# Hashed attention with a maxout feed-forward: four heads per transposed tile, scores in 32-row rounds

## The chip, the cores and the metric

The kernel runs on one core of a Trainium2 chip. The time is that of the device for one launch, in microseconds (us); each kernel was run several times. Engines: PE is TensorE (matmuls), PEld its weight loads, DVE is VectorE, ACT is ScalarE, POOL is GpSimd, SP issues DMAs. A run is called slow when it is over 1.5% above the fastest of the same kernel; ratios use fast runs alone. A ratio is the mean time of one kernel's fast runs over the mean time of the kernel before in the same rounds on the same chip, so it is not quite the ratio of the medians that stand beside it.

## The reference, cut to what matters

```python
# q, k, v: (4 batches, 8 heads, 768, 64), proj: (64, 6)
q_bits = (q @ proj) > 0; k_bits = (k @ proj) > 0      # six bits a row
mask   = all six bits of the two rows agree
scores = where(mask, q @ k.T / 8, -1e9); attn = softmax(scores) @ v
x = attn of all heads side by side                     # (3072, 512)
h = max(x @ w1, x @ w2, x @ w3); out = h @ w_out       # 768 hidden, 512 out
```

## The kernel before

A batch has two groups of four heads (`pp`), and each group two halves of 384 queries: four phases a batch, 16 in all. A phase has six groups `c` of 128 keys. In each, PE makes the scores of four heads, and one more matmul a head adds a large negative number wherever the hash bits differ. ACT takes the exp. In the next phase PE sums the exps (`den`) and multiplies them by v (`av`). Feed-forward pieces of the batch before (`l1`, `l2`) are put between the groups. PSUM is the memory that PE writes its results to, and it is used in banks. The program gives a bank out anew once another engine has read out what stood in it. `scp` holds three tiles of two PSUM banks each for the scores, and `wkp` holds two PSUM banks for all that isn't scores or hash bits: `den`, `av`, `l1` and `l2` take turns in them.

```python
    scp = ... tile_pool(name="scp", bufs=3, space=PSUM)   # scores, two banks each
    wkp = ... tile_pool(name="wkp", bufs=2, space=PSUM)   # all else, one bank each

    def qk_group(ph, b, pp, half, c):
        for jj in (0, 1):                        # two heads a tile: 64 rows each
            for hd in (0, 1):
                nc.tensor.matmul(sc[:, hd, 0:HS], kT[D*hd : D*hd+D, ...], qT[D*hd : D*hd+D, ...],
                                 start=True, stop=False)
        for jj in (0, 1):
            for hd in (0, 1):                    # hash bits: 32 rows each
                nc.tensor.matmul(scs[jj][:, hd, 0:HS], bits["k", b, pp][32*g : 32*g+32, ...],
                                 bits["q", b, pp][32*g : 32*g+32, ...], start=False, stop=True)
        ... nc.scalar.activation(..., ActFn.Exp, scale=SCALE)

    def den(ph, b, pp, half):
        ... # 24 matmuls with ones into one bank
        nc.vector.tensor_scalar(out=ds[:], in0=ps[:, 0:HS], ...)       # frees the bank
        nc.vector.transpose(dT..., ds[:]); nc.vector.reciprocal(rc[:], dT[:, :, 0])
        for jj in (0, 1):
            ... nc.gpsimd.tensor_copy(r2[o : o+32, :], rc[s : s+32, :])   # four of them
            nc.vector.transpose(rb..., r2[:, :, None].to_broadcast(...))  # waits for GpSimd
            rcb[ph, jj] = rb                     # used by av, three groups later

    def l1(b, half, fb, m):
        ... # four matmuls into one bank
        if m == 0: nc.scalar.copy(h[:], ps[:, 0:HS])
        else:      nc.vector.tensor_tensor(out=h[:], in0=h[:], in1=ps[:, 0:HS], op=AluOp.max)
```

The softmax here doesn't subtract the row's maximum and nothing guards it: scores larger than these inputs give would overflow.

## Time and profile before

| stage (by the first exp of each batch) | us |
|---|---|
| launch to the first exp | 24.8 |
| batch 0 | 59.2 |
| batches 1, 2 and 3 to the last exp | 103.2 + 88.4 + 54.4 = 246.0 |
| last exp to the end | 45.1 |
| span of the profiled run | 375.1 |
| median of 2 runs | 377.82 |

The stages are read from the timeline of the 192 exp instructions, 48 a batch. The last stage holds a burst of 15 us of feed-forward as well, since the last exp comes before it.

### The profile page before, as it was taken

The numbers are of one execution on the slowest core, as the hardware profiler recorded it, in microseconds if no ns is written. First come the engines' busy times: TensorE is split into PE (matmuls) and PEld (weight loads), VectorE is DVE, ScalarE is ACT, GpSimd is POOL, SyncE is SP. The second block draws the span as 40 slices with busy tenths as digits, with TensorE's granted clock in tenths as the row PEclk, the third lists the DMA queues.
The fourth block names the chain that finished last, engine by engine and source line by source line (L and its number), as shares of the span: only waits on it lengthen the run. The fifth ranks groups of instructions, "written<-read, shape, count | busy, mean of one in ns | idle before, by whom it ended". The sixth has DMA issues, their size and how long they took to land.

```text
span 375.1 us, 6377 instructions
## 1 busy us (share of the span) xinstructions
PE 304.2 (81%) x2512; PEld 125.8 (34%) x2512; DVE 177.9 (47%) x301; ACT 182.6 (49%) x265; POOL 40.4 (11%) x178
## 2 busy tenths in 40 slices
PE   1278868678989879699988986399989889999796
PEld 0012323223433333235433432134533333345352
DVE  3330857864342576644234448825423535343451
ACT  1037658425657552242377664243276676642122
POOL 8000311101030111000013020100010010100100
PEclk9995799989999996899989999789998999999999
DMA  8999999994032970010199931010020000010202
GB/s 194 234 235 237 237 239 235 235 232 78 2 42 96 232 130 1 2 56 31 56 238 226 230 59 21 0 59 28 2 87 0 2 0 2 33 54 7 78 1 85
DMA packets 16414, 37.64 MB, mean 100 GB/s; under 512 B 2816, under 2 KB 9216, under 8 KB 16384
## 3 DMA queue, kind: packets, MB, share of 16 engines
q1 hardware_dynamic: 9600, 30.94, 33.5%
q0 software_dynamic: 6784, 6.30, 10.8%
q8 instruction: 19, 0.31, 0.4%
q14 instruction: 11, 0.09, 0.1%
HBM read 37.23 MB, written 6.29 MB: 116 GB/s over the span
## 4 chain that ended last, share of the span: by engine, by line
PE 52%; DMA 21%; DVE 14%; issue 6%; POOL 3%; ACT 2%; SPq 1%; DVEq 0%; POOLq 0%; ACTq 0%
DMA qnat<-in_q_dram 21%; PE wk L255 20%; PE wk L269 8%; PE wk L238 7%; PE sc L184 6%; PE wk L210 4%; PE sc L192 4%; PE bps L160 2%; DVE dT L216 1%; DVE ds L214 1%; DVE xT L245 1%; DVE kb L167 1%; SPq L75 1%; ACT at_145 L197 1%; DVE rc L218 1%
## 5 line engine op out<-in xcount | busy, mean ns | idle before, releaser
L255 PE MATMUL wk<-xT,w_sb 128*128 128x384 f16 x576 | 111.9, 330 | 18.9 <-DVE h_1691 L264 3.7
L255 PEld LDWEIGHTS <-w_sb 128*128 128x128 f16 x576 | 52.1, 98 | 71.5 <-issue 34.6
L192 PE MATMUL sc<-qb,kb 32*128 32x384 bf16 x384 | 34.7, 351 | 1.1 <-DVE qb L167 1.1
L214 DVE TENSOR_SCALAR ds<-wk 128x384 f32<-128x384 f32 x16 | 8.9, 558 | 50.3 <-PE wk L210 50.3
L272 ACT COPY o<-wk 128x512 f32<-128x512 f32 x24 | 14.1, 586 | 36.1 <-PE wk L269 29.6
L242 DVE TENSOR_SCALAR sv<-wk 128x1 f32<-128x1 f32 x32 | 5.0, 157 | 47.1 <-PE wk L238 47.1
L238 PEld LDWEIGHTS <-v 128*64 128x64 f16 x384 | 20.5, 116 | 14.2 <-issue 6.4
L197 ACT ACTIVATE at_137<-sc 128x768 f16<-128x768 f32 x8 | 6.6, 823 | 28.8 <-PE sc L192 28.5
L192 PEld LDWEIGHTS <-kb 32*128 32x128 bf16 x384 | 9.9, 92 | 31.5 <-issue 31.5
L197 ACT ACTIVATE at_181<-sc 128x768 f16<-128x768 f32 x8 | 6.5, 815 | 16.3 <-PE sc L192 16.3
L210 PEld LDWEIGHTS <-ones_131 128*32 128x32 f16 x384 | 9.7, 101 | 13.4 <-issue 9.9
L83 POOL DMA_DIRECT2D v<-in_v_dram x16 | 11.5, 726 | 19.0 <-PE wk L238 19.0
L167 DVE TENSOR_SCALAR qb<-bps,thrq 128x768 bf16<-128x768 f32 x8 | 7.9, 1015 | 10.1 <-PE bps L160 10.1
L197 ACT ACTIVATE at_153<-sc 128x768 f16<-128x768 f32 x8 | 6.5, 814 | 10.6 <-PE sc L192 10.6
L197 ACT ACTIVATE at_173<-sc 128x768 f16<-128x768 f32 x8 | 6.5, 814 | 7.6 <-PE sc L192 7.5
L197 ACT ACTIVATE at_165<-sc 128x768 f16<-128x768 f32 x8 | 6.5, 814 | 7.2 <-PE sc L192 7.2
L160 PE MATMUL bps<-kT_185,pmk 64*32 64x384 f32 x8 | 3.0, 843 | 8.3 <-DVE kT_185 L142 8.3
L216 DVE STREAM_TRANSPOSE dT<-ds 128x384 f32<-128x384 f32 x16 | 9.3, 578 | 0.6
L197 ACT ACTIVATE at_177<-sc 128x768 f16<-128x768 f32 x8 | 6.5, 815 | 4.7 <-PE sc L192 4.6
L197 ACT ACTIVATE at_141<-sc 128x768 f16<-128x768 f32 x8 | 6.5, 814 | 4.6 <-PE sc L192 4.6
L184 PE MATMUL sc<-qT_191,kT_189 64*128 64x384 bf16 x24 | 5.3, 430 | 3.9 <-ACT at_165 L197 0.6
L160 PE MATMUL bps<-kT_189,pmk 64*32 64x384 f32 x8 | 2.8, 844 | 6.9 <-DVE kT_189 L142 6.9
(526 smaller groups left out, 681.5 us busy)
## 6 DMA issues: line engine op xcount, KB each, us to landing
knat<-in_k_dram SPq DMA_DIRECT2D x64, 188.0 KB, 8.0
qnat<-in_q_dram SPq DMA_DIRECT2D x64, 188.0 KB, 8.0
out_dram<-o SPq DMA_DIRECT2D x24, 256.0 KB, 2.0
v<-in_v_dram POOLq DMA_DIRECT2D x16, 192.0 KB, 11.0
w_sb<-in_moe_w_dram POOLq DMA_DIRECT2D x3, 768.0 KB, 45.0
wo_sb<-in_moe_w_out_dram POOLq DMA_DIRECT2D x1, 768.0 KB, 72.1
pr<-in_proj_dram POOLq DMA_DIRECT2D x2, 1.5 KB, 4.1
```

The lines of the kernel that those rows point to most:

```text
L160: nc.tensor.matmul(pst[pp][32 * g : 32 * g + 32, half, 0:HS], pm[nm][D * hd : D * hd + D, :], tr[nm, b, 2 * pp + jj][D * hd : D * hd + D, ...
L167: nc.vector.tensor_scalar(out=t[:].rearrange("p (a n) -> p a n", a=2), in0=pst[pp][:, :, 0:HS], scalar1=thr[nm][:, 0:1], scalar2=(1.0 if n ...
L184: nc.tensor.matmul(sc[:, hd, 0:HS], kT[D * hd : D * hd + D, c * P : c * P + P], qT[D * hd : D * hd + D, half * HS : half * HS + HS], start ...
L192: nc.tensor.matmul(scs[jj][:, hd, 0:HS], bits["k", b, pp][32 * g : 32 * g + 32, c * P : c * P + P], bits["q", b, pp][32 * g : 32 * g + 32, ...
L197: nc.scalar.activation(atile(ph, jj, c)[:, :, 0:HS], scs[jj][:, :, 0:HS], ActFn.Exp, scale=SCALE)
L210: nc.tensor.matmul(ps[32 * g : 32 * g + 32, 0:HS], ones32[:], atile(ph, jj, c)[:, hd, 0:HS], start=(c == 0), stop=(c == NCH - 1))
L214: nc.vector.tensor_scalar(out=ds[:], in0=ps[:, 0:HS], scalar1=float(S) * EPS, scalar2=None, op0=AluOp.add)
L216: nc.vector.transpose(dT[:].rearrange("p a x -> p (a x)"), ds[:])
L238: nc.tensor.matmul(ps[D * hd : D * hd + D, 0 : HS + 1], vv[:, hd, c, :], atile(ph, jj, c)[:, hd, :], start=(c == 0), stop=(c == NCH - 1))
L255: nc.tensor.matmul(ps[:, 0:HS], w_sb[m][:, jc, fb * P : fb * P + P], xT[b][:, jc, half * HS : half * HS + HS], start=(jc == 0), stop=(jc = ...
L269: nc.tensor.matmul(ps[:, 0:DM], hts[b, half, fb][:, t * P : t * P + P], w_sb[3][:, fb, :], start=(fb == 0), stop=(fb == NFB - 1))
L272: nc.scalar.copy(o[:], ps[:, 0:DM])
```

## The change

The intent: four heads share one transposed tile, each head in one group of 32 rows, with its 64 numbers in two rounds; the hash bits are a third round of the same form. So all twelve matmuls of a score group have one form. The tile is loaded as it lies in memory, once. Seven parts of it are told apart below: loads halved; a quicker start (half loads, and 14 dummy matmuls while they run); what follows from these for batch 0; 32-row rounds; transposes spread over slots; the first of three maxima copied by DVE; and all PSUM banks used at the end.

```diff
-                nc.sync.dma_start(t[32*g : 32*g+32, 0 : R*D-32], s[:, 32*blk : 32*blk + R*D-32])   # x4 a pair of heads
+            nc.sync.dma_start(t[:], src)                       # four heads, once; halves for the first tile
-    nc.gpsimd.dma_start(pr[0:D, :], proj[:, :])
-    nc.gpsimd.dma_start(pr[D : 2*D, :], proj[:, :])
+    for g in range(4):
+        nc.scalar.dma_start(pr[32*g : 32*g+32], proj.rearrange("(a d) n -> d a n", a=2))
...
+        for rnd in range(3):
+            for g in range(4):
+                rows = slice(32*g, 32*g+32)
+                if rnd < 2: l, r = kT[rows, rnd, ks], qT[rows, rnd, qs]
+                else:       l, r = bits["k", b, pp][rows, ks], bits["q", b, pp][rows, qs]
+                nc.tensor.matmul(scs[g//2][:, g%2, 0:HS], l, r, start=(rnd == 0), stop=(rnd == 2))
...
     def bank():
+        if tail["on"]:
+            m = tail["i"] % 4
+            if m == 1: tail["t"] = scp.tile([P, 2, 512], ...); return tail["t"][:, 0, :]
+            if m == 2: return tail["t"][:, 1, :]
         return wkp.tile([P, 512], FP32, tag="wk", name="wk")[:]
...
-            nc.scalar.copy(h[:], ps[:, 0:HS])
+            if tail["on"]: nc.scalar.copy(h[:], ps[:, 0:HS])
+            else:          nc.vector.tensor_copy(h[:], ps[:, 0:HS])
...
-    (transposes of the next batch: four in a row at two places)
+            slots = [(1, 4), (1, 5), (2, 1), (2, 5), (3, 0), (3, 1), (3, 2), (3, 3)]   # (phase, group), one each
```

The hash now runs on 32 x 32 tiles, up to sixteen at once. To let them, three of four results come out shifted by whole groups of 32 rows, and small DMAs from SBUF to SBUF shift them back.

More of the change, by code (lines that the diff above doesn't have):

```diff
@@ L49 @@
     konst = ctx.enter_context(tc.tile_pool(name="konst", bufs=1))
-    natp = ctx.enter_context(tc.tile_pool(name="natp", bufs=4))
+    natp = ctx.enter_context(tc.tile_pool(name="natp", bufs=2))
     tp = ctx.enter_context(tc.tile_pool(name="tp", bufs=3))
@@ L66, with load @@
     nat = {}
-    def load_pair(b, j):
-        for nm, src in (("k", k), ("q", q)):
-            t = natp.tile([P, R * D], FP32, tag=nm + "nat", name=nm + "nat")
-            for hd in (0, 1):
-                for blk in (0, 1):
-                    g = 2 * hd + blk
-                    s = src[b, 2 * j + hd].rearrange("(i r) d -> i (r d)", r=R)
-                    nc.sync.dma_start(t[32 * g : 32 * g + 32, 0 : R * D - 32],
-                                      s[:, 32 * blk : 32 * blk + R * D - 32])
-            nat[nm, b, j] = t
+    def load(nm, b, pp, half=None):
+        src = {"k": k, "q": q}[nm][b, 4 * pp : 4 * pp + 4].rearrange("h (i r) d -> (h i) (r d)", r=R)
+        if (nm, b, pp) not in nat:
+            nat[nm, b, pp] = natp.tile([P, R * D], FP32, tag=nm + "nat", name=nm + "nat")
+        t = nat[nm, b, pp]
+        if half is None:
+            nc.sync.dma_start(t[:], src)
+        else:
+            cs = slice(NT3 * half, NT3 * half + NT3)
+            nc.sync.dma_start(t[:].rearrange("p (jj c d) -> p jj c d", jj=4, d=D)[:, :, cs, :],
+                              src.rearrange("p (jj c d) -> p jj c d", jj=4, d=D)[:, :, cs, :])
     vt = {}
     def load_v(b, j):
-        t = vp.tile([P, 2, S // P, D], FP16, tag="v", name="v")
+        t = vp.tile([P, 2, NCH, D], FP16, tag="v", name="v")
         nc.gpsimd.dma_start(
@@ L86, in load_v @@
         vt[b, j] = t
-    pr = konst.tile([P, NBITS], FP32, name="pr")
-    load_pair(0, 0)
-    nc.gpsimd.dma_start(pr[0:D, :], proj[:, :])
-    nc.gpsimd.dma_start(pr[D : 2 * D, :], proj[:, :])
-    load_pair(0, 1)
+    pr = konst.tile([P, 2, NBITS], FP32, name="pr")
+    for g in range(4):
+        nc.scalar.dma_start(pr[32 * g : 32 * g + 32], proj.rearrange("(a d) n -> d a n", a=2))
+    load("k", 0, 0, 0)
+    load("q", 0, 0, 0)
+    load("k", 0, 0, 1)
+    load("q", 0, 0, 1)
     load_v(0, 0)
     load_v(0, 1)
+    warm = konst.tile([P, 512], BF16, name="warm")
+    nc.vector.memset(warm[:], 0.0)
     thr = {}
@@ L105 @@
         thr[nm] = tt
-        m = konst.tile([P, 32], FP32, name="pm" + nm)
+        m = konst.tile([P, 2, 32], FP32, name="pm" + nm)
         nc.vector.memset(m[:], 0.0)
@@ L112 @@
         pos0 = NBITS - neg0
-        nc.vector.tensor_copy(pm[nm][:, pos0 : pos0 + NBITS], pr[:])
-        nc.vector.tensor_scalar(out=pm[nm][:, neg0 : neg0 + NBITS], in0=pr[:], scalar1=-1.0,
+        nc.vector.tensor_copy(pm[nm][:, :, pos0 : pos0 + NBITS], pr[:])
+        nc.vector.tensor_scalar(out=pm[nm][:, :, neg0 : neg0 + NBITS], in0=pr[:], scalar1=-1.0,
                                 scalar2=None, op0=AluOp.mult)
@@ L136, with transpose @@
     tr = {}
-    def transpose(nm, b, j):
-        n = nat.pop((nm, b, j))
-        pp, jj = divmod(j, 2)
-        t = tp.tile([P, S], FP32, tag=f"{nm}T{jj}", name=f"{nm}T{jj}")
+    def transpose(nm, b, pp, blk, halves=(0, 1)):
+        n = nat[nm, b, pp]
+        if (nm, b, pp) not in tr:
+            tr[nm, b, pp] = tp.tile([P, 2, S], FP32, tag=nm + "T", name=nm + "T")
+        t = tr[nm, b, pp]
+        c0, c1 = NT3 * halves[0], NT3 * halves[-1] + NT3
         nc.vector.transpose(
-            t[:].rearrange("p (c i jj) -> p jj c i", jj=4, i=32),
-            n[:].rearrange("p (r x) -> p r x", x=D)[:, :, 0:32])
-        tr[nm, b, j] = t
+            t[:, blk, c0 * P : c1 * P].rearrange("p (c i jj) -> p jj c i", jj=4, i=32),
+            n[:].rearrange("p (jj c x) -> p jj c x", jj=4, x=D)[:, :, c0:c1, 32 * blk : 32 * blk + 32])
@@ L147, with hash_bits @@
     bits = {}
-    def group(pp, jj, hd):
-        return (2 * hd + jj) if pp == 0 else (2 * (1 - hd) + jj)
-    def hash_bits(nm, b, pps):
-        pst = {pp: scp.tile([P, 2, 512], FP32, tag="sc", name="bps") for pp in pps}
-        for half in (0, 1):
-            for pp in pps:
-                for jj in (0, 1):
-                    for hd in (0, 1):
-                        g = group(pp, jj, hd)
-                        nc.tensor.matmul(
-                            pst[pp][32 * g : 32 * g + 32, half, 0:HS],
-                            pm[nm][D * hd : D * hd + D, :],
-                            tr[nm, b, 2 * pp + jj][D * hd : D * hd + D, half * HS : half * HS + HS],
-                            start=True, stop=True)
-        for pp in pps:
-            t = tp.tile([P, S], BF16, tag=nm + "b", name=nm + "b")
-            nc.vector.tensor_scalar(
-                out=t[:].rearrange("p (a n) -> p a n", a=2), in0=pst[pp][:, :, 0:HS],
-                scalar1=thr[nm][:, 0:1], scalar2=(1.0 if nm == "q" else MISS),
-                op0=AluOp.is_gt, op1=AluOp.mult)
-            bits[nm, b, pp] = t
+    def hash_bits(specs, half):
+        cs = slice(half * HS, half * HS + HS)
+        pst = []
+        for i in range(0, len(specs), 2):
+            ps = scp.tile([P, 2, 512], FP32, tag="sc", name="bps")
+            pst += [ps[:, 0, 0:HS], ps[:, 1, 0:HS]]
+        for blk in (0, 1):
+            for (nm, b, pp, sh), ps in zip(specs, pst):
+                for g in range(4):
+                    o = 32 * ((g + sh) % 4)
+                    nc.tensor.matmul(ps[o : o + 32, :], pm[nm][32 * g : 32 * g + 32, blk, :],
+                                     tr[nm, b, pp][32 * g : 32 * g + 32, blk, cs],
+                                     start=(blk == 0), stop=(blk == 1))
+        for (nm, b, pp, sh), ps in zip(specs, pst):
+            if (nm, b, pp) not in bits:
+                bits[nm, b, pp] = tp.tile([P, S], BF16, tag=nm + "b", name=nm + "b")
+            t = bits[nm, b, pp]
+            d = t[:, cs]
+            if sh:
+                x = tp.tile([P, HS], BF16, tag="bx", name="bx")
+                d = x[:]
+            nc.vector.tensor_scalar(out=d, in0=ps, scalar1=thr[nm][:, 0:1],
+                                    scalar2=(1.0 if nm == "q" else MISS), op0=AluOp.is_gt, op1=AluOp.mult)
+            if sh:
+                m = 32 * sh
+                nc.sync.dma_start(t[0 : P - m, cs], x[m:P, :])
+                nc.sync.dma_start(t[P - m : P, cs], x[0:m, :])
@@ L177, in qk_group @@
     def qk_group(ph, b, pp, half, c):
-        scs = []
-        for jj in (0, 1):
-            sc = scp.tile([P, 2, 512], FP32, tag="sc", name="sc")
-            kT = tr["k", b, 2 * pp + jj].bitcast(BF16)[:, 1::2]
-            qT = tr["q", b, 2 * pp + jj].bitcast(BF16)[:, 1::2]
-            for hd in (0, 1):
-                nc.tensor.matmul(sc[:, hd, 0:HS],
-                                 kT[D * hd : D * hd + D, c * P : c * P + P],
-                                 qT[D * hd : D * hd + D, half * HS : half * HS + HS],
-                                 start=True, stop=False)
-            scs.append(sc)
-        for jj in (0, 1):
-            for hd in (0, 1):
-                g = group(pp, jj, hd)
-                nc.tensor.matmul(scs[jj][:, hd, 0:HS],
-                                 bits["k", b, pp][32 * g : 32 * g + 32, c * P : c * P + P],
-                                 bits["q", b, pp][32 * g : 32 * g + 32, half * HS : half * HS + HS],
-                                 start=False, stop=True)
+        scs = [scp.tile([P, 2, 512], FP32, tag="sc", name="sc") for _ in (0, 1)]
+        qs = slice(half * HS, half * HS + HS)
+        ks = slice(c * P, c * P + P)
+        kT = tr["k", b, pp][:].bitcast(BF16).rearrange("p a (n two) -> p a n two", two=2)[:, :, :, 1]
+        qT = tr["q", b, pp][:].bitcast(BF16).rearrange("p a (n two) -> p a n two", two=2)[:, :, :, 1]
+        for rnd in range(3):
+            for g in range(4):
+                rows = slice(32 * g, 32 * g + 32)
+                if rnd < 2:
+                    l, r = kT[rows, rnd, ks], qT[rows, rnd, qs]
+                else:
+                    l, r = bits["k", b, pp][rows, ks], bits["q", b, pp][rows, qs]
+                nc.tensor.matmul(scs[g // 2][:, g % 2, 0:HS], l, r, start=(rnd == 0), stop=(rnd == 2))
         for jj in (0, 1):
             nc.scalar.activation(atile(ph, jj, c)[:, :, 0:HS], scs[jj][:, :, 0:HS], ActFn.Exp, scale=SCALE)
+    tail = {"on": False, "i": 0, "t": None}
     def bank():
+        if tail["on"]:
+            tail["i"] += 1
+            m = tail["i"] % 4
+            if m == 1:
+                tail["t"] = scp.tile([P, 2, 512], FP32, tag="sc", name="tl")
+                return tail["t"][:, 0, :]
+            if m == 2:
+                return tail["t"][:, 1, :]
         return wkp.tile([P, 512], FP32, tag="wk", name="wk")[:]
@@ L260, in l1 @@
             hts[b, half, fb] = h
-            nc.scalar.copy(h[:], ps[:, 0:HS])
+            if tail["on"]:
+                nc.scalar.copy(h[:], ps[:, 0:HS])
+            else:
+                nc.vector.tensor_copy(h[:], ps[:, 0:HS])
         else:
@@ L284 @@
     ffn = deque()
-    def prep(b, pp):
-        for j in (2 * pp, 2 * pp + 1):
-            for nm in ("k", "q"):
-                transpose(nm, b, j)
-    prep(0, 0)
-    hash_bits("k", 0, [0])
-    hash_bits("q", 0, [0])
-    load_pair(0, 2)
-    load_pair(0, 3)
+    wps = wkp.tile([P, 512], FP32, tag="wk", name="wps")
+    for _ in range(14):
+        nc.tensor.matmul(wps[:], warm[:, 0:P], warm[:], start=True, stop=True)
+    for half in (0, 1):
+        for nm in ("k", "q"):
+            transpose(nm, 0, 0, 0, (half,))
+            transpose(nm, 0, 0, 1, (half,))
+            if half == 0:
+                hash_bits([(nm, 0, 0, 0)], 0)
+    for nm in ("k", "q"):
+        load(nm, 0, 1)
     load_v(0, 2)
@@ L301 @@
     for ph, (b, pp, half) in enumerate(phases):
-        todo = {}
+        todo = {c: [] for c in range(NCH)}
         if prev is not None:
-            todo[0] = [lambda a=prev: den(*a)]
-            todo[3] = [lambda a=prev: av(*a, 0)]
-            todo[4] = [lambda a=prev: av(*a, 1)]
-        if b == 0 and pp == 0 and half == 1:
-            todo.setdefault(1, []).append(lambda: prep(0, 1))
-            todo.setdefault(4, []).append(lambda: hash_bits("k", 0, [1]))
-            todo.setdefault(5, []).append(lambda: hash_bits("q", 0, [1]))
+            todo[0].append(lambda a=prev: den(*a))
+            todo[3].append(lambda a=prev: av(*a, 0))
+            todo[4].append(lambda a=prev: av(*a, 1))
@@ new lines @@
+        n = 2 * pp + half
+        if ph == 0:
+            todo[1].append(lambda: hash_bits([("k", 0, 0, 0)], 1))
+            todo[3].append(lambda: hash_bits([("q", 0, 0, 0)], 1))
+        if ph == 1:
+            for i, (nm, blk) in enumerate((("k", 0), ("k", 1), ("q", 0), ("q", 1))):
+                todo[i].append(lambda nm=nm, blk=blk: transpose(nm, 0, 1, blk))
+            sp = [("k", 0, 1, 0), ("q", 0, 1, 1)]
+            todo[4].append(lambda: hash_bits(sp, 0))
+            todo[5].append(lambda: hash_bits(sp, 1))
@@ L311 @@
         if b + 1 < B:
             nb = b + 1
-            if pp == 0 and half == 1 or (pp == 1 and half == 0):
-                def ld(p2=(0 if pp == 0 else 1)):
-                    for j in (2 * p2, 2 * p2 + 1):
-                        load_pair(nb, j)
-                        load_v(nb, j)
-                todo.setdefault(2, []).append(ld)
-            if pp == 1 and half == 0:
-                todo.setdefault(5, []).append(lambda: prep(nb, 0))
-            if pp == 1 and half == 1:
-                todo.setdefault(1, []).append(lambda: prep(nb, 1))
-                todo.setdefault(4, []).append(lambda: hash_bits("k", nb, [0, 1]))
-                todo.setdefault(5, []).append(lambda: hash_bits("q", nb, [0, 1]))
@@ L325 @@
-        ngroups_left = (NPP * 2 - (pp * 2 + half)) * NCH
+            if n in (0, 2):
+                p2 = n // 2
+                todo[2].append(lambda p2=p2: (load("k", nb, p2), load("q", nb, p2)))
+            if n in (1, 3):
+                p2 = n // 2
+                todo[0].append(lambda p2=p2: (load_v(nb, 2 * p2), load_v(nb, 2 * p2 + 1)))
+            if n == 2 and b > 0 or n == 3 and b == 0:
+                pass
+            lst = [(nm, p2, blk) for p2 in (0, 1) for nm in ("k", "q") for blk in (0, 1)]
@@ new lines @@
+            slots = [(1, 4), (1, 5), (2, 1), (2, 5), (3, 0), (3, 1), (3, 2), (3, 3)]
+            for (nm, p2, blk), (nn, c) in zip(lst, slots):
+                if nn == n:
+                    todo[c].append(lambda nm=nm, p2=p2, blk=blk: transpose(nm, nb, p2, blk))
+            if n == 3:
+                sp = [("k", nb, 0, 0), ("q", nb, 0, 1), ("k", nb, 1, 2), ("q", nb, 1, 3)]
+                todo[4].append(lambda: hash_bits(sp, 0))
+                todo[5].append(lambda: hash_bits(sp, 1))
@@ L326 @@
+        ngroups_left = (NPP * 2 - n) * NCH
         for c in range(NCH):
             qk_group(ph, b, pp, half, c)
-            for f in todo.get(c, []):
+            for f in todo[c]:
                 f()
@@ L331 @@
                 rest = sum(a[0] for a in ffn)
-                if pp == 0 and half == 0 and c <= 4:
+                if n == 0 and c <= 4:
                     rest += 15.5
@@ L342 @@
         prev = (ph, b, pp, half)
+    tail["on"] = True
     den(*prev)
```

## The prediction

> **What bounds the kernel now.** I read the page first: row 2 (the slices), then the busy time by stage, then the chain of waits, then the timeline where a stage loses time.
>
> ```profile
> PE   1278868678989879699988986399989889999796
> PEclk9995799989999996899989999789998999999999
> DMA  8999999994032970010199931010020000010202
> GB/s 194 234 235 237 237 239 235 235 232 78 2 42 96 232 130 1 2 56 31 56 238 226 230 59 21 0 59 28 2 87 0 2 0 2 33 54 7 78 1 85
> ```
>
> One slice is 9.4 us. For nine slices (to 84 us) the DMA engines are full at about 236 GB/s and never again for long; in that time PE is the least busy. So the kernel has two regimes. The exp instructions of the scores come in 16 phases of six groups (four phases a batch); phase 0 starts at 24.8 us, batch 1 at 84.0, batch 2 at 187.2, batch 3 at 275.7, the last sums at 348. By these stages (columns: stage, busy us of PE, PEld, DVE, ACT, POOL, clock, DMA share, GB/s):
>
> ```profile
> 24.00:84.00 60.00, 44.95 (x440) 15.57 (x444) 34.71 (x46) 36.39 (x48) 7.26 (x28) 0.86 1.14 236
> 84.00:186.00 102.00, 89.59 (x709) 37.99 (x702) 50.48 (x85) 49.36 (x74) 8.76 (x36) 0.95 0.29 64
> 186.00:275.00 89.00, 73.78 (x633) 31.02 (x632) 43.99 (x72) 45.24 (x67) 8.76 (x36) 0.94 0.42 97
> 275.00:348.00 73.00, 67.64 (x572) 29.40 (x572) 29.20 (x60) 45.17 (x67) 5.95 (x32) 0.98 0.06 23
> 348.00:375.00 27.00, 20.43 (x138) 10.32 (x130) 10.52 (x21) 5.14 (x10) 1.49 (x8) 1.00 0.14 50
> ```
>
> Batch 0 waits for loads (the chain that ended last runs through the q loads, 21% of it); batches 1 to 3 are PE with waits; the tail is PE alone. Batches 2 and 3 hold the same matmuls (31 us of feed-forward each), but batch 2 also prepares the next batch: 89 against 73 us, so **preparing costs 16 us**. The waits of 222 to 246 us say why:
>
> ```profile
> PE wk L269 <- DVE h_2703 L264: 6.4, 1, 6.4
> PE wk L210 <- DVE h_2607 L264: 3.3, 1, 3.3
> ```
>
> Four input transposes (1.4 us apart) stand ahead of those DVE maxima in DVE's order; only two PSUM banks serve den, av and feed-forward, so PE stops for 3.3 and 6.4 us. How the scores run, from the timeline:
>
> ```profile
> 59.70 0.34 PE L184 MATMUL sc<-qT_390,kT_388 64*128 64x384 bf16 x2
> 59.88 0.33 PE L184 MATMUL sc<-qT_394,kT_392 64*128 64x384 bf16 x2
> 60.15 0.34 PE L192 MATMUL sc<-qb,kb 32*128 32x384 bf16 x4
> 60.42 0.34 PE L184 MATMUL sc<-qT_390,kT_388 64*128 64x384 bf16 x2
> ```
>
> Two 64-row matmuls, or four 32-row ones, start together. Start to start is 0.18 us inside the 64-row form, 0.27 at each change of form: a group costs 0.72 us.
>
> **What the Trainium skill says.** "TensorEngine Tiling (Array Packing)", section Tiling Modes: "Changing tiling mode (not just tile) drains the TensorE". The rows above agree: 0.27 against 0.18, about 0.10 us for a change. "TensorE: Matmul & The Clock Gate", section Why this matters for your kernels: a 32-row matmul takes as long as a 128-row one, the gain is that tiles run together; the four of L192 do (0.34 us each, one start). So two rounds of four 32-row tiles should equal the two pairs of 64-row tiles; the contraction gains nothing by itself. Same section: a gap of over about 3 us lets the array fall to half clock. Agrees: after the 6.4 us wait the L269 matmuls come 0.43 us apart, elsewhere 0.216, and the clock of 240 to 250 us was 0.68. "DMA: Bandwidth & Descriptors", section Queues, rings and completion order: an engine alternates between queues packet by packet; so the weights' queue can slow the smaller-packet first loads. No row of the kernel before isolates that.
>
> **The change, part by part.**
>
> 1. *Loads.* Before, 32 partitions take one 32-wide half of a head by loading nearly the whole head, so each head is read twice: 128 loads of 188 KB for q and k. After, one 768 KB load holds four heads once: half the bytes. Row 3 of the page gives the cost: queue q1 33.5% of 375.1 us for 30.94 MB, 4.06 us per MB; q0 10.8% for 6.30 MB, 6.4 us per MB. Due before batch 1: before, 12.3 MB of q and k and 4.7 MB of weights and v, 50 + 30 = 80 us (seen: 84). After, 6.3 MB, 26 + 30 = 56 us. Loads stop bounding batch 0 if it lasts longer than that.
>
> 2. *Start.* First exp now: 24.8 us; PE waits 8.3 us for the first k transpose and the last of four full tiles is transposed at 18.9. After, half a tile (393 KB, about 2 us at 200 GB/s behind a first landing that took 2.8 us) allows: k half at about 4.5 us, two half transposes of 0.8, the fp32 hash matmuls 1.5, their compare 0.6, then the same for q: 4.5 + 1.6 + 1.5 + 0.6 + 1.6 + 1.5 + 0.6 + 0.7 of scores = 12.6. First exp at 12.6 to 13, 12 us earlier. The 14 dummy matmuls fill PE time that is idle anyway.
>
> 3. *Batch 0.* An undisturbed phase takes 10.2 us (phase 2: 51.96 to 62.16), about 1.6 a group: an exp of 0.81, then the scores that wait for its bank, 0.71. Phases 1 and 3 took 16.8 and 21.8 because transposes and hash came in a lump behind late loads. After: 13 + phase 0 with two half hashes (10.2 + 3) + phase 1 with two (10.2 + 4.5) + 10.2 + phase 3 with two hashes of four tiles, their eight compares and the copies that shift bits (10.2 + 5.5) = 66.8. Against 84.0: **minus 17** (12 of them at the start).
>
> 4. *Scores in 32-row rounds.* 0.16 + 0.16 + 0.27 = 0.60 instead of 0.72: a change of form less per group. 384 more matmuls and weight loads, but four start together. Of the 72 groups of batches 1 to 3 some 60 are PE-bound (at the head of a batch exp bounds): 60 x 0.115, **minus 7**. In batch 0 nothing; the chain from a free bank to exp has a round more and a change less.
>
> 5. *Transposes spread.* Same 32 full transposes of 1.4 us, now one or two at a slot over three phases. Of the 16 us: hash matmuls 2.9 (stay; 16 tiles of 32x32 in place of 8), their bank waits 2 (stay), the 3.3 and 6.4 us waits, half clock 2. Eight separate waits of about 0.5 us stay: 9 instead of 16, twice (batches 1 and 2): **minus 13**, rounded down a little. Shift copies hide behind 15.5 us of feed-forward at a batch's end, save after batch 0.
>
> 6. *First of three maxima copied by DVE, not ACT.* 42 copies leave ACT (0.48 us) for DVE (about 0.55). It ends waits behind two exps, but in dense feed-forward the bank's round trip sets the pace (0.73 us for four matmuls against 0.65) and grows by 0.07, and DVE goes from 178 to about 200 busy us: 42 x 0.07, **plus 3**.
>
> 7. *All banks at the end.* The last 72 L255 matmuls take 13.4 us, 0.186 each; with free banks 0.1625 each, 11.7; and 0.3 of the 2.68 us wait for a bank: **minus 2**.
>
> Sum: 377.8 - 17 - 7 - 13 + 3 - 2 = 341.8, say **342**.
>
> **Rivals.** *(a) The loads stay the bound of batch 0*: strided first loads of 768-byte pieces share engines with v and weights; the second halves land at 16 us instead of 10, and weights late. For it: q0 moved only about 0.06 MB/us while q1 was busy. Against: 56 us of work against a need at 67. It would make 350. *(b) DVE becomes the bound of batches 1 and 2*: in batch 2 DVE is busy 44 of 89 us; plus copies, and the stage shorter, 50 of 75. In order, every transpose ahead of a bank's release stalls PE. It would give back 6 to 10: 350. *(c) Preparation disappears wholly*, DVE slots falling into slack: 6 more gained in each of two batches: 330. *(d) The 12 matmuls and 12 weight loads of a group cannot issue fast enough*: plus 5 to 10. Against: den already issues four loads and four matmuls in 0.16 us.
>
> **Range and chances.** Most of the sum is bytes and waits that I can see: 17 + 7 + 2 are fairly safe, 13 - 3 less so. Single rivals move it by 8 to 12, so 330 to 354 holds it 8 times in 10. Faster by over 2% needs only 8 of the 36 us: 0.96. Within 2%: 0.03, slower: 0.01, for a cost that I do not see, as in rival (d).
>
> **What would show it.** Right: first exp near 13 us; DMA full to about 55 us, not 84; batch 1 starting near 67; a group's matmuls 0.16 us apart and 0.60 in all; no PE wait over 2 us for a DVE maximum and no slice of clock 0.7 in the middle; batches 2 and 1 shorter by some 10 and 9 us, batch 3 by 1 to 3; last matmuls 0.163 apart. Wrong: batch 1 starting after 75 us (a), PE waiting for DVE copies in many small pieces (b), starts of the three rounds more than 0.2 us apart (d).

## The result, and the profile after

The changed kernel took 364.64 us (median of 2, 364.46 to 364.82): the ratio to before is 0.9651 (0.961 to 0.9693). It is faster, by 13 us. The prediction had said 342, 36 us less, and a range that ends at 354.

The page of the kernel after, the rows of its 40 slices (9.1 us each; the clock and the DMA share in tenths as before):

```profile
PE   5688688669797886989898795979998897999685
PEclk9689999899989996999989999899999998999999
DMA  8999243132025103130563003111200000102002
```

The DMA engines are full for four slices only, to 36 us, where they were full for nine. By stage (columns: stage, busy us of PE, PEld, DVE, ACT, POOL, clock, DMA share, GB/s):

```profile
17.20:74.60 57.40, 43.96 (x660) 16.55 (x657) 38.77 (x57) 35.86 (x48) 7.21 (x28) 0.93 0.56 132
74.60:176.90 102.30, 88.50 (x884) 39.46 (x886) 61.27 (x107) 41.47 (x57) 8.71 (x36) 0.95 0.23 68
176.90:260.80 83.90, 72.17 (x795) 32.08 (x796) 50.98 (x88) 39.53 (x55) 8.71 (x36) 0.96 0.25 74
```

Batch 0 isn't bound by loads any more (a DMA share of 0.56, where it was 1.14), and yet it is only 1.8 us shorter. In batch 1 DVE has 61 busy us where it had 50, and the stage is as long as before. Against the prediction:

| stage | before | predicted | after | missed by |
|---|---|---|---|---|
| to the first exp | 24.8 | 12.6 | 17.2 | 4.6 |
| batch 0 | 59.2 | 54.2 | 57.4 | 3.2 |
| batches 1 to 3 | 246.0 | 229.0 | 240.6 | 11.6 |
| last exp to the end | 45.1 | 43.1 | 47.8 | 4.7 |

(The prediction's 66.8 us for the start of batch 1 less its 12.6 makes 54.2; for the three batches its terms -7, -13 and +3 are taken from 246.0.)

One part is as predicted. A score group of the timeline after, with what follows it:

```profile
279.38 0.52 PE L202 MATMUL sc<-qT,kT 32*128 32x384 bf16 x8
279.73 0.33 PE L202 MATMUL sc<-qb,kb 32*128 32x384 bf16 x4
279.99 0.35 PE L255 MATMUL wk<-at_129,v 128*64 128x385 f16 x2
```

Eight matmuls in two rounds, then the hash bits after 0.35 us, then the next form: 0.61 us in all where it was 0.72.

The rest is waits. PE's waits in batch 1, first before and then after (columns: who waits, for whom; us in total, times, longest us):

```profile
PE wk L255 <- DVE h_1691 L264: 3.7, 1, 3.7
PE wk L210 <- DVE h_1595 L264: 2.8, 1, 2.8
PE wk L255 <- DVE h_1434 L264: 1.6, 1, 1.6
PE wk L255 <- DVE h_967 L264: 1.6, 1, 1.6
PE wk L255 <- DVE h_1192 L264: 1.6, 1, 1.6
```

```profile
PE wk L272 <- DVE h_1882 L281: 3.8, 1, 3.8
PE wk L272 <- DVE h_1118 L281: 2.4, 1, 2.4
PE wk L272 <- DVE h_1620 L281: 2.4, 1, 2.4
PE wk L272 <- DVE h_1375 L281: 2.4, 1, 2.4
```

L281 is the new copy on DVE. At the heads of three phases of this batch PE now waits 2.4 us for it, and at the fourth 3.8; before, it waited 1.6 us for a maximum at three of them (the 3.7 and the 2.8 stand behind the lumps of transposes). In batches 2 and 3 the copy makes PE wait over 2 us only once each, 3.8 and 2.4 us. What DVE does ahead of that copy is in its timeline (start us, length us; in brackets the idle time ahead of the row and what ended it):

```profile
77.01 0.23 DVE L235 RECIPROCAL rc<-dT 128x12 f32<-128x12 f32 x1
78.27 0.58 DVE L244 STREAM_TRANSPOSE rb_1104<-r_1099 128x384 f32<-128x384 f32 x1 [1.04 <-POOL r_1099 L242]
79.20 0.58 DVE L244 STREAM_TRANSPOSE rb_1111<-r_1106 128x384 f32<-128x384 f32 x1 [0.35 <-POOL r_1106 L242]
79.71 0.52 DVE L281 CAST h_1118<-wk 128x384 f16<-128x384 f32 x1
80.33 0.55 DVE L284 TENSOR_TENSOR h_1118<-h_1118,wk 128x384 f16<-128x384 f16 x1
```

DVE works in the program's order. After the reciprocal (77.2) it stands idle until GpSimd has copied the first four pieces (1.04 us), makes one transpose, is idle again (0.35), and makes the other. Only then, at 79.71, does it come to the copy, 2.5 us after the reciprocal: 1.4 us of it idle and 1.1 the two transposes. PE's matmuls for it had started at 75.7. In the two waits of 3.8 us one of the spread input transposes (1.5 us) stands ahead of the copy as well. The results of those two transposes aren't wanted until `av`, three groups later. I had not seen in the profile before that the 1.6 us waits were this.

### The profile page after: what moved, and what is told of

Same layout as the page of the kernel before. It is cut to its first block, busy times and chain, and to the rows that moved or that the text cites. A ratio compares the mean times of both kernels' runs of the same rounds, so it can differ in the third digit from the quotient of the medians.

```text
span 363.1 us, 7556 instructions
## 1 busy us (share of the span) xinstructions
PE 300.6 (83%) x3166; PEld 131.1 (36%) x3166; DVE 203.4 (56%) x364; ACT 162.3 (45%) x223; POOL 39.1 (11%) x176
## 5 line engine op out<-in xcount | busy, mean ns | idle before, releaser
L272 PE MATMUL wk<-xT,w_sb 128*128 128x384 f16 x540 | 107.2, 334 | 30.2 <-DVE h_1882 L281 3.8
L272 PEld LDWEIGHTS <-w_sb 128*128 128x128 f16 x576 | 53.1, 98 | 89.8 <-issue 58.4
L202 PE MATMUL sc<-qT,kT 32*128 32x384 bf16 x768 | 59.8, 344 | 10.9 <-DVE bx L178 2.3
L202 PEld LDWEIGHTS <-kT 32*128 32x128 bf16 x768 | 15.1, 94 | 53.2 <-issue 48.6
L167 PE MATMUL bps<-qT,pmq 32*32 32x384 f32 x256 | 21.6, 552 | 5.8 <-DVE sv L259 4.3
L167 PE MATMUL bps<-kT,pmk 32*32 32x384 f32 x256 | 20.8, 553 | 5.9 <-DVE kT L150 4.0
L150 DVE STREAM_TRANSPOSE kT<-knat 128x768 f32<-128x768 f32 (+1 forms) x18 | 25.1, 1437 | 0.0
L150 DVE STREAM_TRANSPOSE qT<-qnat 128x768 f32<-128x768 f32 (+1 forms) x18 | 24.7, 1387 | 0.0
L204 ACT ACTIVATE at_127<-sc 128x768 f16<-128x768 f32 x8 | 6.5, 815 | 18.7 <-PE sc L202 18.6
L204 ACT ACTIVATE at_159<-sc 128x768 f16<-128x768 f32 x8 | 6.5, 814 | 18.7 <-PE sc L202 18.7
L204 ACT ACTIVATE at_171<-sc 128x768 f16<-128x768 f32 x8 | 6.5, 814 | 16.0 <-PE sc L202 15.9
L178 DVE TENSOR_SCALAR kb<-bps,thrk 128x384 bf16<-128x384 f32 x10 | 6.2, 617 | 12.8 <-PE bps L167 12.8
L167 PEld LDWEIGHTS bps<-kT,pmk 32*32 32x32 f32 x256 | 6.7, 110 | 14.3 <-DVE kT L150 5.0
L85 POOL DMA_DIRECT2D v<-in_v_dram x16 | 11.6, 726 | 0.8 <-POOLq L400 0.8
L204 ACT ACTIVATE at_143<-sc 128x768 f16<-128x768 f32 x8 | 6.5, 814 | 11.4 <-PE sc L202 11.4
```

The costliest lines, as they stand in the source:

```text
L85: nc.gpsimd.dma_start(t[:].rearrange("p h c d -> p h (c d)"), v[b, 2 * j : 2 * j + 2].rearrange("h (p c) d -> p h (c d)", p=P))
L150: nc.vector.transpose(t[:, blk, c0 * P : c1 * P].rearrange("p (c i jj) -> p jj c i", jj=4, i=32), n[:].rearrange("p (jj c x) -> p jj c x", ...
L167: nc.tensor.matmul(ps[o : o + 32, :], pm[nm][32 * g : 32 * g + 32, blk, :], tr[nm, b, pp][32 * g : 32 * g + 32, blk, cs], start=(blk == 0) ...
L178: nc.vector.tensor_scalar(out=d, in0=ps, scalar1=thr[nm][:, 0:1], scalar2=(1.0 if nm == "q" else MISS), op0=AluOp.is_gt, op1=AluOp.mult)
L202: nc.tensor.matmul(scs[g // 2][:, g % 2, 0:HS], l, r, start=(rnd == 0), stop=(rnd == 2))
L204: nc.scalar.activation(atile(ph, jj, c)[:, :, 0:HS], scs[jj][:, :, 0:HS], ActFn.Exp, scale=SCALE)
```

## The experiments

Seventeen kernels were run, all with correct results. Each was timed beside the kernel before (medians of 376 to 378 us on these chips). Stage lengths are from the profiled run, and those of e4, e6, e7, e10, e11 and e12 come from slow runs. A stage's length holds two things, how long PE waits and how fast its clock is; where they matter, PE's idle and busy time of batches 1 to 3 are given, for the same matmuls. Line numbers differ between the kernels, since the edits add lines.

**Run e1_hact: the copy back on ACT.**

```diff
-            if tail["on"]: nc.scalar.copy(h[:], ps[:, 0:HS])
-            else:          nc.vector.tensor_copy(h[:], ps[:, 0:HS])
+            nc.scalar.copy(h[:], ps[:, 0:HS])
```

> Part 6 undone: the first of three maxima is copied by ScalarE again. Theory A (the copy on VectorE lengthens the waits for a bank, because it stands behind the sums' transposes in VectorE's order): about 359 (357 to 361), and the PE waits of 2.4 us at the heads of phases fall to about 1.6. Rival B (the place of the copy is indifferent, VectorE would hold the bank with the next maximum anyway): 364 to 365. Rival C (ScalarE's exps then hold the copies up): over 366.

Measured: 358.57 us, ratio 0.9526 (after: 0.9651). Batches 1 to 3 took 230.5 us instead of 240.6. The copies, predicted at +3, had cost 10 us of these three batches by the profile: PE's idle time there fell from 32.2 to 26.3 us (the waits of 2.4 us to 1.7) and its busy time from 208.5 to 204.2, with batch 1 at a clock of 1.00 instead of 0.95. The time as a whole fell by 6 us. Theory A.

**Run e2_notail: two banks at the end.**

```diff
-        if tail["on"]:
+        if False:          # in bank()
```

> Part 7 undone: two banks at the end as before, copies there on ScalarE as in both kernels. Theory A (the two halves of a shared tail tile come free only together, so the extra banks cost more than they give): last stage 45 us instead of 47.8, about 361.5. Rival B (the end is longer for another reason, for example the clock after a wait): 364 to 365.

Measured: 362.92 us, ratio 0.9631 (0.9571 to 0.9691), which isn't told apart from after by the time; the last stage alone was 46.3 us instead of 47.8, where theory A had asked for 45. A cause of this part shows in the waits of the kernel after from the last exp on:

```profile
PE tl L272 <- DVE h_4490 L284: 0.7, 1, 0.7
PE tl L289 <- DVE h_4563 L284: 0.7, 1, 0.7
PE tl L272 <- DVE h_4545 L284: 0.7, 1, 0.7
PE tl L272 <- DVE h_4472 L284: 0.7, 1, 0.7
```

`tl` is the tile whose two banks serve two pieces in turn; PE waits for it 0.7 us again and again, because it can be used anew only when both banks are empty.

**Run e3_proj: the four proj loads on GpSimd's queue.**

```diff
-        nc.scalar.dma_start(pr[32*g : 32*g+32], ...)
+        nc.gpsimd.dma_start(pr[32*g : 32*g+32], ...)
```

> The four small proj loads go out on GpSimd's queue instead of ScalarE's, nothing else. Theory A (the start waits for proj, which landed at 8.7 us): first exp at about 13 to 14 us instead of 17.2, 361 in all. Rival B (they land as late on any queue, as they share engines with the q and k loads; or the k half is next in line anyway): 364 to 365.

The first exp came at 14.9 us instead of 17.2. Proj was there only 0.7 us sooner (8.0 instead of 8.7); most of the rest is PE's clock, 1.00 up to the first exp instead of 0.82: its q hash took 1.54 us instead of 2.78. No gain shows in the time: 364.07 to 371.22, with two of four runs slow (ratio of the fast ones 0.981, verdict unclear). Part of theory A, in the profile alone.

**Run e4_laterb: the two transposes that wait for GpSimd, issued two groups later.**

```diff
     def den(ph, b, pp, half):
         ... # sums, reciprocal and GpSimd's copies as before
+    def den2(ph):                                 # the two transposes
+        for jj in (0, 1): nc.vector.transpose(rb..., r2...); rcb[ph, jj] = rb
...
             todo[0].append(lambda a=prev: den(*a))
+            todo[2].append(lambda a=prev: den2(a[0]))
```

> The two transposes that wait for GpSimd's copies of the reciprocals are issued two groups later, so that nothing stands behind that wait in VectorE's order. Theory A (PE's waits of 2.4 us at phase heads are this wait handed on through the banks): those waits fall under 1 us in eight phases, about 357 (355 to 360). Rival B (the waits come from VectorE's amount of work): 363 to 365.

Measured: 336.36 us median, the three fast runs 335.62 to 336.70, ratio 0.8922: 28 us faster than after, nearly four times what theory A had asked for. The profiled run was the slow one of the four (341.45), and even in it batches 1 to 3 took 213.1 us instead of 240.6. In DVE's timeline the copy now follows the reciprocal at once, and the transposes, two in a row, wait for nothing:

```profile
78.76 0.23 DVE L236 RECIPROCAL rc<-dT 128x12 f32<-128x12 f32 x1
78.91 0.50 DVE L287 CAST h<-wk 128x384 f16<-128x384 f32 x1
...
81.51 1.03 DVE L250 STREAM_TRANSPOSE rb<-r 128x384 f32<-128x384 f32 x2
```

PE's longest waits in batch 1 are now these:

```profile
PE wk L278 <- DVE h L287: 2.6, 2, 1.3
PE wk L261 <- DVE h L290: 1.1, 1, 1.1
```

Nothing was removed; only the place of the two transposes changed. So the waits at the heads of the phases were the two transposes with their in-order wait for GpSimd, handed on to PE through the two banks. How much of it is the idle 1.4 us and how much the 1.1 us of the transposes themselves, no run parts, since both moved. The mean clock of the fast runs rose too, from 0.952 and 0.958 to between 0.974 and 0.984. In the profiled runs the two can be told apart for batches 1 to 3: PE's idle time fell from 32.2 to 13.3 us, and its busy time from 208.5 to 199.8 as the clock rose from 0.95 to 0.97 up to 1.00. So some 19 us are waits that went and 9 us faster matmuls. That the clock rose because the waits went is likely but not shown.

**Run e5_before_laterb: the same edit in the kernel before.**

> The kernel before, with only the two reciprocal transposes issued two groups later. Theory A (the in-order wait for GpSimd was there before, and the change made it cost more by putting the copies behind it too): 12 waits of 1.5 us go, about 362 (358 to 367), a gain half of the 28 us that the same edit gave after the change. Rival B (the change made this wait): 375 to 378. Rival C (the wait was there as large before, so the change's own parts are worth as little with it gone as with it): about 349.

Measured: 356.45 us, ratio 0.9468, a gain of 20 us, more than theory A's range and less than rival C's figure. The wait was in the kernel before as well. With it gone from both, the change is worth 356.5 to 336.0, 20 us; with it in both, 13.

**Run e6_laterb_hact_notail: e4 with the copy on ACT and two banks at the end.** The edit is those of e4, e1 and e2 together.

> After, with the transposes later (336.4 measured), and parts 6 and 7 undone together. Theory A (with nothing standing behind the wait the copy on VectorE is nearly free, and the tail banks cost 2 to 3): about 334. Rival B (the copy is a loss by itself, as its undoing alone gave 6): 329 to 331. Rival C (the copy now helps, as it was meant to): 336 to 340.

Fast runs 327.26 and 330.25 (ratio 0.873), the other two slow. Both profiled runs, this and e4's, are slow ones: batches 1 to 3 210.0 us against e4's 213.1, the end 46.5 against 50.1. By these stages the copies cost about 3 us once the in-order wait is gone, as predicted, and the tail's banks about as much. But two slow runs are compared, and by the total (the two fast runs are 6 to 9 us under e4's 336.0) it is nearest to rival B, 329 to 331, and not theory A. That the copy alone is cheap then rests on e16 below.

**Run e7_laterb_lump: e4 with the input transposes in fours.**

```diff
-            slots = [(1, 4), (1, 5), (2, 1), (2, 5), (3, 0), (3, 1), (3, 2), (3, 3)]
+            slots = [(2, 5), (2, 5), (2, 5), (2, 5), (3, 1), (3, 1), (3, 1), (3, 1)]
```

> After, with the reciprocal transposes later and the input transposes lumped in fours as before the change (part 5 undone). Theory A (spreading is worth what the prediction said, 13 us in two batches, once the other wait is gone): about 349, all in the batches before the last. Rival B (the waits of 3.3 and 6.4 us were mostly the reciprocal chain's too): 336 to 340.

One fast run of 349.98, three slow ones to 359.31, so no ratio. In the profiles, slow in both, batches 1 and 2 were 96.4 and 83.7 us against 89.8 and 75.9 in e4, and batch 3, which prepares nothing, 47.4 in both. That is 14.4 us for spreading; the prediction had 13. Here too some of it is the clock, 0.96 in both batches against 1.00 in e4. The one fast run is 14 us above e4's fast ones as well.

**Run e12_lump: after with the transposes in fours, the wait for GpSimd left in.** The edit is that of e7.

> After with only part 5 undone (input transposes lumped in fours). Theory A (with the in-order wait for GpSimd in place the spread transposes' gain was partly used up): 370 to 375, less than the 14 to 20 that lumping cost with that wait gone. Rival B (the gain of spreading was whole): 378 or over. Rival C (spreading gave nothing here): 363 to 366.

The two fast runs took 380.81 and 382.31 (ratio 1.0145): 17 us more than after by the mean times and 19 by the ratios, rival B. Spreading gave no less with the other wait in place; theory A was wrong. A third run took 389, and one, the profiled one, 925.69 us: its L272 matmuls took 951 ns where they take 326, with DVE's busy time the same (204.0 us) and the recorded clock at 1.00. No reading rests on it.

**Run e8_twice: every q and k load made a second time, into a tile that nobody reads.**

```diff
             nc.sync.dma_start(t[:], src)
+            t2 = dup.tile([P, R * D], FP32, ...); nc.sync.dma_start(t2[:], src)    # likewise for the halves
```

> After, with each q and k load made a second time into a tile that nobody reads, so that the bytes are those of before. Theory A (batch 0 isn't bound by loads any more; its transposes and hashes on VectorE bind it): start later by 3 to 5 us, batch 0 itself as long within 3 us, 367 to 371 in all. Rival B (bytes bound batch 0 and their halving made the gain): batch 0 longer by 8 or more, 376 or over.

374.03 us, ratio 0.9932: 9 us more than after, between what A and B had asked for. Batch 0 grew by 8.7 us to 66.1, as rival B said. But its first exp came 2.7 us sooner (14.5 us: proj landed 1.1 us sooner, and the clock from 10 to 20 us was 0.84 instead of 0.55), so batch 1 began only 5.9 us later, at 80.5 instead of 74.6. That is what the halved bytes are worth up to there; 2.8 of the 8.8 us between the two profiled runs lie in batch 3 and the end, where no q or k is loaded, and aren't explained.

**Runs e9_best, e10_early and e11_tail1.** All have e4's and e1's edits and load proj first on the queue of the q and k loads. e9 has two banks at the end. e10 is e9 with two of batch 0's transposes a phase earlier. e11 has five banks at the end that come free one by one.

```diff
-        nc.scalar.dma_start(pr[32*g : 32*g+32], ...)
+        nc.sync.dma_start(pr[32*g : 32*g+32], ...)          # all three
+            if b == 0: slots[4:6] = [(2, 4), (2, 5)]         # e10
-            m = tail["i"] % 4 ...
+            m = tail["i"] % 5                                # e11
+            if m in (1, 2, 4): return scp.tile([P, 2, 512], ...)[:, 0, :]
```

> Transposes later, parts 6 and 7 undone, and proj loaded first on the queue of the q and k loads. Theory A (the start waits for proj, delayed by the loads that share its engines): first exp at 13 to 15 us instead of 18, fast runs 325 to 327. Rival B (the k half is as late as proj, since proj's loads now stand ahead of it): first exp at 17 or later, 328 to 330.

> As the run before it, with two of the four k transposes... that is, both halves of the last k tile of batch 0 transposed a phase earlier. Theory A (in batch 0 the hash of the next batch waits for the transposes in VectorE's order): batch 0 shorter by 2 to 4 us than in the run before it. Rival B (the clock, the exps and the matmuls of the hash set the length): within 1 us.

> As the first of these runs, with the end on five banks of which each comes free alone (one bank used of each score tile). Theory A (the tail of the change was slow because two banks came free together): last stage 1 to 2 us shorter than with two banks, the last feed-forward matmuls 0.163 us apart. Rival B (more banks can't help, the engines that empty them set the pace): within 0.5 us of two banks, or longer.

e9: fast runs 328.15 to 332.65, ratio 0.8796, no faster than e6; proj was there at 5.6 us, but DVE then waited 4.0 us for the k half, and the first exp came at 19.2 us. Rival B: the one was gained and the other lost. e10: ratio 0.8775, the same; batch 0 was 60.5 us against e9's 56.7, and its transposes now waited for their data, as DVE's waits of the first 76 us show:

```profile
DVE kT L150 <- DMA knat<-in_k_dram: 6.3, 2, 5.5
```

So it told nothing of theory A. e11: one fast run of 326.28, three slow ones to 334.36, no ratio; its last stage (in a slow run) took 45.3 us against e9's 46.5, and late in the feed-forward there the pieces of four matmuls start 0.65 us apart, 0.163 a matmul. Theory A by the profile.

**Run e13_start: after with another start.**

```diff
+        (nc.sync if g % 2 == 0 else nc.scalar).dma_start(pr[32*g : 32*g+32], ...)
...
+    hold = konst.tile([P, 6144], FP32, name="hold")
+    nc.gpsimd.memset(hold[:], 0.0)                # GpSimd issues the v and weight loads after this
     load_v(0, 0)
```

> After, with proj's four loads split over two hardware queues ahead of the k halves and the v and weight loads held back by a GpSimd memset of about 5 us; nothing else. Theory A (the start is later than predicted because proj and the halves share the DMA engines with v and the weights): first exp at 12.5 to 14.5 us instead of 17.2, about 361. Rival B (the in-order start on VectorE or the half clock keeps it): first exp at 16 or later.

360.55 us, ratio 0.9549. The first exp came at 12.4 us: theory A, and the prediction's 12.6. DVE's first row on proj in the kernel after, and then, from this run, the first k transpose and the first exps:

```profile
8.68 0.17 DVE L119 COPY pmq<-pr 128x12 f32<-128x12 f32 x1 [6.50 <-DMA pr<-in_proj_dram]
```

```profile
5.47 0.87 DVE L153 STREAM_TRANSPOSE kT<-knat 128x384 f32<-128x384 f32 x1
...
12.43 2.96 ACT L207 ACTIVATE at<-sc 128x768 f16<-128x768 f32 x4 [9.48 <-PE sc L205]
```

In the kernel after, proj landed last. PE's dummy matmuls ended at 5.9 us, PE then had nothing until 9.9, and from 10 to 20 us its clock was 0.55, so that the q hash took 0.64 us a pass where it takes 0.32. With the loads in this order the clock was 1.00 throughout the start. Two things were changed at once, proj's queues and the hold on v and the weights; which of them counts isn't parted. Beside GpSimd's memset of 5.2 us DVE's four small rows on proj took 2.6 to 2.8 us each, where they take 0.17; it cost nothing here, since the k half came only at 5.4 us.

**Run e14_all: e4, e1, e11's five banks and e13's start together.**

> All that helped together: reciprocal transposes later, copy on ScalarE, end on five single banks, and this start. If the gains add, fast runs at 321 to 325; if the start's gain is lost again before batch 1, 326 to 329.

325.07 us (322.18 to 325.87, four fast runs), ratio 0.8597, at the edge of what adding gains had asked for. This beats both kernels: 40 us under the changed kernel and 52 under the one before. Batches 1 to 3 took 207.8 us with a clock of 1.00, the end 43.4.

**Runs e15_before_dvecopy and e16_before_laterb_dvecopy: the copy on DVE as the only change to the kernel before, and the same with the two transposes later.**

```diff
-            nc.scalar.copy(h[:], ps[:, 0:HS])
+            if tail["on"]: nc.scalar.copy(h[:], ps[:, 0:HS])
+            else:          nc.vector.tensor_copy(h[:], ps[:, 0:HS])
```

> The kernel before with part 6 alone: the first of three maxima copied by VectorE outside the end. Theory A (the copy stands behind the sums' in-order wait for GpSimd and hands it on to PE): 6 to 10 us slower than before, 383 to 387. Rival B (it costs only the longer round trip of the bank, as predicted): 379 to 381. Rival C (it helps, as ScalarE's exps held the copies): under 377.

> The same with the reciprocal transposes two groups later (356.4 without the copies on VectorE). Theory A (with nothing behind that wait, the copy costs the 3 us that were predicted): 358 to 361. Rival B (the copy's cost is VectorE's load itself): 363 or over.

e15: 386.85 us, ratio 1.0242 (1.0193 to 1.0292), 9 us slower than before. Its waits in batch 1 on the copy:

```profile
PE wk L257 <- DVE h L266: 7.9, 4, 2.3
```

Four waits for the copy (L266 here) of up to 2.3 us, where there were three of 1.6 for a maximum. PE's idle time in batches 1 to 3 rose from 32.8 to 37.9 us, its busy time from 213.2 to 219.5 (clock of batch 1 0.89 instead of 0.95). e16: 358.20, ratio 0.9482, against e5's 356.45 and 0.9468: by these medians the copy costs 2 us once nothing stands behind the wait for GpSimd. Theory A in both.

**Run e17_early2: e14 with batch 0's next loads and two transposes a phase earlier.**

```diff
+            if b == 0 and n == 1: todo[3].append(lambda: (load("k", nb, 1), load("q", nb, 1)))
+            if b == 0: slots[4:6] = [(2, 4), (2, 5)]
```

> The run with everything together (325.1), and for batch 0 alone the next batch's second pair of loads issued a phase earlier, ahead of the shift copies, so that two of its four transposes can be made a phase earlier without waiting for their data. Theory A (the hash at the end of batch 0 waits for transposes in VectorE's order): batch 0 about 55 to 56.5 us instead of 58.9, 322 to 323 in all. Rival B (clock, exps and the hash's own matmuls set batch 0): 58 to 60, about 325.

329.21 us (327.47 to 330.54), ratio 0.8725; batch 0 took 58.6 us against e14's 58.9. Rival B: the place of those transposes doesn't set batch 0. That this run was 4 us slower than e14 comes from later stages (batches 2 and 3 and the end, 5.9 us together), which the edit doesn't touch; the clock there was 0.98, 0.97 and 0.95 where e14 had 1.00. Why it was lower stays unexplained; it shows that a few us between runs of separate rounds mean little here.

## Why the prediction was wrong

The direction was right and the size was not: 13 us instead of 36. By its own steps:

1. **Loads: right in what they bound.** They stopped binding batch 0 (share 0.56), and e8 shows that their bytes are worth 6 us by the start of batch 1 and 9 in all.
2. **Start: mis-sized.** The term was 12 us and measured 7.6. "k half at about 4.5 us" was sound (it landed at 4.7); left out was proj, which the changed kernel loads by four DMAs on ACT's queue and which was there only at 8.7 us (before, by two on GpSimd's queue, at 6.2), and the half clock that came after PE's 4 us without work. e13 sets both right and gets 12.4. That this is so near 12.6 is partly luck: there the first k transpose began at 5.5 us and not at 4.5, but each hash began before its second transpose was done, which the sum did not count on.
3. **Batch 0: mis-sized, cause open.** Predicted 5 us shorter, measured 1.8. In the kernel after, PE's hash waits behind DVE's transposes and sums in phases 1 and 3, but e17 moved transposes away and gained nothing. In the late-transpose kernels a wait for a shift copy shows at the head of a phase (2.7 us in e14). What sets the 57 us isn't shown.
4. **Scores: right by the group.** 0.61 us a group instead of 0.72. The 7 us that this should give were not tested: no run puts the old rounds back.
5. **Spread transposes: right in kind, a little low.** 13 predicted; 14 in e7, 17 to 19 in e12. No wait of 6.4 us is left; the longest in batches 1 to 3 is 3.8. (The term took batch 2's waits of 3.3 and 6.4 us for batch 1 too, where they were 2.8 and 3.7.)
6. **The copies: the step that failed.** "It ends waits behind two exps" and "42 x 0.07, plus 3" counted the copy's own length. e1 measured 10 us in batches 1 to 3 (6 of PE's idle time, 4 of its busy time) and 6 in all; e15 measured 9 in the kernel before. What I had left out is what stands ahead of the copy in DVE's order: the two transposes that wait for GpSimd. On ACT the copy had freed one of two banks without passing them, so PE could go one piece further; this last is read from the order of the code. e16 (2 us) shows that the copy alone costs no more than I had said, once that wait is away; e6's stages (about 3, in slow runs) agree, its total does not. Of the 11.6 us missed in batches 1 to 3, this term is 7 by e1's stages and 3 by its total.
7. **The end: wrong sign.** Predicted 2 us shorter, measured 2.7 longer; the shared tile of two banks makes PE wait. Two banks as before give back 1.5 us (e2: 46.3 against 47.8), five single ones gain 1.2 more over two (e11: 45.3 against e9's 46.5). The other 1.2 us of the 2.7 stay open.

The wait itself was in the kernel before, where it stood as "DVE h L264: 1.6" in the waits. I had put PE's waits for DVE down to the lump of transposes, which was right for 3.3 and 6.4 us and wrong for these. The rest of the miss in batches 1 to 3, 4 us or more, I put to this wait as well, since the change is worth 20 us without it in either kernel (e5, e4) and 13 with it; that last split is argued, not shown. Of the rivals, (b) came nearest: its "every transpose ahead of a bank's release stalls PE" is what happened, and its 6 to 10 us fit e1. But it was put down to DVE's amount of work, and the transposes that mattered most were the two that wait for GpSimd: e4 leaves DVE as much to do (135 busy us in batches 1 to 3, where it had 138) and loses the waits.

## What to carry to other kernels

When an engine that works in order waits for another engine, everything behind it waits too, and the profile charges the wait to the instruction that came last, not to the one that was stuck. Look at the idle brackets in that engine's timeline. Issue an instruction that has to wait shortly before its result is used, not where its inputs are made. Before work is moved to an engine, read what stands ahead of it there: the same copy cost 6 to 10 us behind such a wait and 2 to 3 without.

## What the Trainium skill lacked or had wrong

- "TensorE: Matmul & The Clock Gate", in its table of specifications, says that VectorE's queue is strictly first in, first out. It doesn't say what that costs: here 1.4 us of idle time on VectorE at the head of a phase, with 1.1 us of the two transposes that had waited, handed on through two PSUM banks, was worth 28 us of 364 when these two were issued later (run e4_laterb; some 19 of it idle time of TensorE, 9 its matmuls at a higher clock), and 20 of 377 in the kernel before.
- "TensorEngine Tiling (Array Packing)", section Tiling Modes, says that a change of form drains the array but gives no figure: here 0.26 to 0.27 us from start to start across a change and 0.16 to 0.18 within a form, for matmuls of 384 columns.
